# A gated recurrence with a highway layer behind it: loads with four instead of eight neighbouring tokens per partition, and another written order

## The chip, the cores and the metric

The kernel runs on one core of one Trainium2 chip. The metric is the device time of one execution in microseconds (us). Before the change the median of three runs is 213.28 us (213.11 to 213.91).

## What is computed

Four sequences of 6,336 tokens with 256 features go through a gated recurrence and then, token by token, through a highway layer:

```
f = lb + (1 - lb) * sigmoid(f_logit)          # lb: one number a feature
h[t] = f[t] * h[t-1] + (1 - f[t]) * x[t]      # one recurrence for each sequence and feature
H = max(h @ w_h, 0);  T = sigmoid(h @ w_t + b_t)
out = T * H + (1 - T) * h                     # [4, 6336, 256] as 25344 rows, float32
```

All inputs and the output are float32 in memory: 26 MB each for x, f_logit and out.

## The kernel before

The work is cut into 25 units. Each of units 0 to 23 is 1,024 tokens (8 blocks of 128) of one sequence; the last one, unit 24, is 192 tokens of each of the four. Units 0 to 2 and 24 enter in smaller pieces (`CUTS`, line 44), so that there are 30 front pieces and 26 back pieces. Pieces are numbered from 0 below.

**Front**, for each piece i. `lt` and `xt` are loaded with tokens on the partitions (line 106). ScalarE makes `u = sigmoid(-lt)` (line 154). GpSimd makes the product `bv = u * xt`, 256 columns of features for two blocks an instruction (lines 160 and 172). TensorE transposes `u` to `uT` (line 198) and `bv` to `bT` (line 215), so that features lie on the partitions and tokens along them; ScalarE makes the decay `f = 1 + ncc * uT` (line 205); VectorE runs the recurrence as a scan, `y = f * y + bT` (line 230).

**Back**, for each unit. TensorE multiplies `y` by the two weight matrices, to `zp` and `gp` (line 245); ScalarE makes `t` (line 251); VectorE makes `d` (line 256); VectorE and GpSimd share the product `e = d * t` (line 166 on VectorE, line 160 on GpSimd; of backs 0 to 2 VectorE makes all of it); TensorE adds `y` and `e` and transposes back, to `op` (lines 296 and 297); ScalarE copies it to `o` (line 303), and in the last three backs VectorE does part of that. `o` is stored (line 309).

**The weights** are loaded raw (line 125, two loads of 256 KB) and scaled once by VectorE into `w_sb` (line 148, two instructions, h = 0 and h = 1, each over both matrices); each reads both `w_raw` and `ndiag` from SBUF.

**Which tokens a load puts on a partition.** `run(piece)` (line 108) tells how many neighbouring tokens go to one partition. With 8, a partition gets 8 tokens as one piece of 8,192 bytes; with 4, it gets two pieces of 4,096 bytes. Pieces of 4 or 2 blocks have a run of 4 or 2 in any case, and the last unit has 2. Line 205 puts the tokens of `f` back in order as it writes, and line 213 does so for `bT`. Stores always use up to 4 tokens, which is 4,096 bytes.

**What sets the order.** `PLAN` (line 349) is a list written out by hand: each letter issues the next step of its kind, and the engines get their instructions in that order. L and X load `lt` and `xt`, Q loads a weight, U is `u`, P the GpSimd product, A and B the transposes of `u` and `bv`, F the decay, S the scan, W the scaling of the weights, Z and G the matrix products, T, D and E the gates and the VectorE part of `e`, H the GpSimd part of it, O the output transposes, C and V the copies on ScalarE and VectorE, R the store. The digit after A, B, Z, G or O is the PSUM slot. All loads and stores go through SyncE's queue in the list's order. In what follows S2.0 is the scan of front piece 2, half 0, W0 and W1 are the two instructions of line 148, and so on. The buffers of `lt` and `xt` are 5 each, those of `o` 8.

Where VectorE makes `e`, the next GpSimd product is made to wait for it (`port`, line 156). Line 148 has no such wait.

Of the kernel before, what the change touches and what calls it, by code (L numbers as in the profile page):

```python
# [19 lines left out]
def kernel(  # L20
# [36 lines left out]
    units = [(P, NB, b, NB, s0) for s0 in range(0, S - rest, NB * P) for b in range(B)]  # L57
# [44 lines left out]
    def load(i, name, src):  # L102
        u, j0, j1 = fronts[i]
        np_, j = units[u][0], run(fronts[i])
        t = fs[i][name] = new(name, [NB, D], FP32)
        pin(nc.sync.dma_start(t[:np_, :j1 - j0].rearrange("p (k j) d -> p k (j d)", j=j), tokens(src, u, j0, j1, j)))

    def run(piece):

        u, j0, j1 = piece  # L110
        return min(8, j1 - j0, units[u][3])

    def shape(piece):

# [86 lines left out]
    def decay_act(i, h):  # L201

        np_, N, j = shape(fronts[i])[0], width(fronts[i]), run(fronts[i])
        f = fs[i]["f", h] = new("f", [NB * P], FP16)
        pin(nc.scalar.activation(f[:, :N].rearrange("p (k q j) -> p k q j", q=np_, j=j),  # L205
                                 fs[i]["uT", h].rearrange("p (k j q) -> p k q j", q=np_, j=j), AF.Identity,
                                 scale=ncc[:, h:h + 1], bias=1.0))

    def b_pe(i, m, slot):
        (np_, nb), r = shape(fronts[i]), run(fronts[i]) // 2  # L210
        for bT, h in filled(fronts[i], m, slot, fs[i], "bT", BF16):

            t = bT.bitcast(FP32).rearrange("p (k q j) -> p k j q", q=np_, j=r)
            for k in range(nb // 2):
                pin(nc.tensor.transpose(t[:, k // r, k % r],  # L215
                                        fs[i]["bv"][:np_, k, h * P:(h + 1) * P].rearrange("p d j -> p (d j)").bitcast(FP32),
                                        ident_f[:np_, :np_]))
# [97 lines left out]
    def halves_of(pieces):  # L315
# [31 lines left out]
    }  # L347

    PLAN = (
        "XLLLXXLXLQQUUA0A1PFFFUFUB0PSSB1A0FFPSSPB1A0XLLXLXXPFUFSSWWPB1A0G0Z1PFFUPSSDPXLLXLB0A1G2Z0PUTFFTPPB1S"  # L350
        "SDUSSEZ1A0G0G2A1DDPFTFFPPZ1A0B1O0O2PSSTFECCUB0Z1B1G0G2SDSDA0Z0TUFTPPPPPPA0G1B1FXLLLXRRXLXDESA0Z0Z2O1"
        "UFTCTB0G0A1O1O2SDPPPFCCB1A0Z1G0O2FTUCB0G1PPPHPSDSEDPA1Z0Z2B0O1FTUCTESA1G0G1B0DDHPPPPSZ2O0O1FUTCCB1SA"
        "0G2Z0B1FDUTPHPPSXXLRLRRRLRXLRRZ1A0G2O0PDTFCEEG1B1A0O2O0UFCCDSG1B0A1Z2Z0SDPHPPPPFTTA1B0O2O1G0HPSFCCZ2"
        "B1A0Z1DUTFTEG0O2PSPLXXRXRRRRDPPHCB1SA0O1G0Z2B1FCUTDEPSG1Z0A0O2FTCPDPPHB1A0Z1G0O2SFTCDEB0Z1A1G0PLLXRR"
        "RRSDPPPUFTO2B0A1Z0G1SHDCFTEO2B0G0Z1A1PPPPCUFTSDHO2B0A1G0Z1SCFTO2B0A1DEPSZ1G0PPPCUFTDHO2B0A1O0G1SCFCD"
        "EZ2B0A1Z0PSTFTPPPG1B1O2A0O0DUCFCSG1Z2A1B0HDELXLLRXRLLRXRRRRRXPSTFPPZ1G0O2B1DTCSZ1G2A0O0PHUFTCDEB1A0G"
        "2Z1O0PSPFTCDPPHB0G1G2A1Z0UFTSA0B1FDEDSPO1O0Z2B0PPCCTPHSO1A1G0Z2B0UFTCDEPSA1G0Z2O1PPDB0FTCSA1Z2G0O1PH"
        "FUCTDELXRRXXRRLRLXXRRRA1B0G0Z1PSFTO2DCB1A0G1Z0O2PPPHSUFCTDEB1A0Z1G2O0PSDFTCB0A1Z1G2SFPPPHDO0B1A0G2ET"
        "UCFPSO1PZ0CDTB1A0Z1G2SFTUHO0A0B1DFG1EPPPPSO2A0CCZ0DFB1O2Z1B0TCUTSESHPPG0A1Z2G1DDRRRRRRRRFFTA1B0O2Z0Z"
        "1FCFSEHTTG2B1G0O1RSDDCO2SRHCZ0G1STRO2TDDEZ0CTERTG1O2O0DVDVCO2CREVO1CRO0RCVRR"  # L360
    )
    assert all(PLAN.count(k) == len(places) for k, (_, places) in kinds.items())
    todo = {k: iter(places) for k, (_, places) in kinds.items()}
# [31 lines left out]
```

## Time and profile before

| | |
|---|---|
| median of three runs | 213.28 us |
| the profiled execution | 213.28 us |
| its span, first to last instruction | 211.4 us |
| VectorE (DVE) busy | 195.3 us, 154 instructions |
| ScalarE (ACT) busy | 193.6 us, 194 instructions |
| TensorE (PE) busy | 186.1 us |
| GpSimd (POOL) busy | 160.9 us |
| moved by DMA | 78.69 MB |

The profile is of one execution. "Busy" is time in which an engine had an instruction running; consecutive instructions of VectorE and ScalarE overlap by about 0.1 us, so that the distance between two starts is a little less than a duration. The profiled execution's time is 1.9 us longer than its span. The profile lists instructions by line, engine and tile, and gives for each group what ended the idle time of the engine before it.

### The profile page before, as it was taken

The page shows a single profiled execution, that of the slowest core. Times are in us where ns is not written, and L with a number is a line of the kernel's source. Part 1 is how long each engine was busy: PE and PEld are TensorE (multiplying, and loading weights), DVE is VectorE, ACT ScalarE, POOL GpSimd, SP SyncE. Part 2 cuts the span into 40 slices and gives each one's busy share as a digit, 9 for nine tenths or more (in the row PEclk, how much of TensorE's full clock was granted, in tenths as well). Part 3 has the DMA queues.
Part 4 walks back from the last instruction along what each step waited for, and adds up shares of the span by engine and source line. Part 5 has one row for each costly group of instructions (what it writes and reads, how often), then busy time and mean ns, then how long its engine had stood idle before and what let it go on. Part 6 is the DMA issues. An engine that isn't in the chain of part 4 may idle for free.

```text
span 211.4 us, 4591 instructions
## 1 busy us (share of the span) xinstructions
PE 186.1 (88%) x1775; PEld 131.5 (62%) x1800; DVE 195.3 (92%) x154; ACT 193.6 (92%) x194; POOL 160.9 (76%) x133
## 2 busy tenths in 40 slices
PE   0559988899898999999999999999999899999980
PEld 0336564477565766776767666668576676865770
DVE  1279999999999999999999999999999999999980
ACT  3677999999999999999999999999999999998750
POOL 4667665988699698978988898898899876866400
PEclk9999999999999999999999999999999999999996
DMA  5999999999999999999999999999999996252465
GB/s 124 414 412 429 430 423 425 426 419 426 425 422 425 415 429 419 425 428 414 425 420 428 422 426 420 423 412 426 418 431 409 360 408 282 98 203 99 198 253 198
DMA packets 17350, 78.69 MB, mean 372 GB/s; under 512 B 2352, under 2 KB 2864, under 8 KB 11952
## 3 DMA queue, kind: packets, MB, share of 16 engines
q1 hardware_dynamic: 16784, 78.39, 90.6%
q8 instruction: 14, 0.23, 0.4%
q10 hardware_dynamic: 544, 0.00, 0.1%
q14 instruction: 8, 0.07, 0.1%
HBM read 52.43 MB, written 25.95 MB: 371 GB/s over the span
## 4 chain that ended last, share of the span: by engine, by line
ACT 36%; PE 25%; issue 13%; DVE 13%; DMA 9%; SPq 1%; POOL 1%; ACTq 1%; DVEq 0%; POOLq 0%
ACT t L251 10%; ACT u L154 9%; ACT f L205 8%; ACT o L303 8%; PE zp L245 7%; DMA out_dram<-o 6%; DVE y L230 6%; PE gp L245 6%; DVE d L256 5%; PE bT L215 4%; PE uT L198 3%; PE op L296 3%; DMA xt<-in_x_dram 3%; PE op L297 3%; DVE e L166 1%
## 5 line engine op out<-in xcount | busy, mean ns | idle before, releaser
L160 POOL TENSOR_TENSOR bv<-u,xt 128x512 bf16<-128x512 f16 (+1 forms) x100 | 114.5, 1176 | 30.7 <-DVE e L166 10.3
L230 DVE TENSOR_TENSOR_SCAN y<-f,y,bT 128x1024 bf16<-128x1024 f16 (+3 forms) x56 | 106.4, 1917 | 2.3 <-ACT f L205 1.3
L205 ACT ACTIVATE f<-uT,ncc 128x1024 f16<-128x1024 f16 (+3 forms) x60 | 65.8, 1109 | 2.4 <-PE uT L198 2.4
L251 ACT ACTIVATE t<-zp,bt 128x1024 bf16<-128x1024 f32 (+1 forms) x52 | 63.7, 1247 | 0.7 <-PE zp L245 0.3
L256 DVE SCALAR_TENSOR_TENSOR d<-y,ncc,gp 128x1024 bf16<-128x1024 bf16 (+1 forms) x52 | 62.4, 1209 | 0.3 <-issue 0.2
L245 PEld LDWEIGHTS <-w_sb 128*128 128x128 f16 x400 | 38.0, 99 | 37.6 <-issue 5.8
L303 ACT COPY o<-op 128x1024 f32<-128x1024 f32 (+2 forms) x50 | 55.6, 1157 | 4.2 <-PE op L297 2.2
L154 ACT ACTIVATE u<-lt 128x2048 f16<-128x2048 f32 (+3 forms) x30 | 53.3, 1779 | 4.2 <-DMA lt<-in_f_logit_dram 4.2
L245 PE MATMUL gp<-y,w_sb 128*128 128x512 bf16 (+1 forms) x187 | 50.6, 382 | 1.5 <-ACT t L251 0.2
L245 PE MATMUL zp<-y,w_sb 128*128 128x512 bf16 (+1 forms) x188 | 49.6, 378 | 1.7 <-DVE d L256 0.6
L296 PE MATMUL op<-diag,y 128*128 128x128 f16 (+1 forms) x400 | 49.2, 219 | 1.9 <-DVE d L256 0.7
L160 POOL TENSOR_TENSOR e<-d,t 128x1024 bf16<-128x1024 bf16 x21 | 44.8, 2132 | 7.4 <-DVE e L166 2.6
L297 PE MATMUL op<-ident_b,e 128*128 128x128 bf16 (+1 forms) x400 | 49.2, 219 | 0.0
L297 PEld LDWEIGHTS <-e 128*128 128x128 bf16 (+1 forms) x400 | 44.7, 114 | 5.6 <-issue 3.4
L296 PEld LDWEIGHTS <-y 128*128 128x128 bf16 (+1 forms) x400 | 44.8, 114 | 2.7
L198 PE MATMUL uT<-ident_h,u 128*128 128x128 f16 (+1 forms) x400 | 32.2, 226 | 9.2 <-ACT u L154 6.4
L198 PEld LDWEIGHTS <-u 128*128 128x128 f16 (+1 forms) x400 | 27.3, 101 | 16.4 <-ACT u L154 6.7
L215 PE MATMUL bT<-ident_f,bv 128*128 128x128 f32 (+1 forms) x200 | 32.3, 284 | 5.0 <-DVE y L230 2.4
L215 PEld LDWEIGHTS bT<-ident_f,bv 128*128 128x128 f32 (+1 forms) x200 | 22.9, 145 | 11.5 <-issue 4.6
L166 DVE TENSOR_TENSOR e<-d,t 128x1024 bf16<-128x1024 bf16 (+2 forms) x26 | 18.9, 734 | 0.1
L230 DVE TENSOR_TENSOR_SCAN y<-f,bT 128x512 bf16<-128x512 f16 (+2 forms) x8 | 10.5, 1338 | 3.3 <-PE bT L215 3.3
L135 DVE TENSOR_SCALAR cc<-lb 128x2 f32<-128x2 f32 x1 | 0.2, 170 | 4.2 <-DMA lb<-in_lower_bound_dram 4.2
(19 smaller groups left out, 10.9 us busy)
## 6 DMA issues: line engine op xcount, KB each, us to landing
out_dram<-o SPq DMA_DIRECT2D x48, 512.0 KB, 13.6
lt<-in_f_logit_dram SPq DMA_DIRECT2D x21, 1024.0 KB, 14.8
xt<-in_x_dram SPq DMA_DIRECT2D x21, 1024.0 KB, 15.8
lt<-in_f_logit_dram SPq DMA_DIRECT2D x5, 512.0 KB, 7.9
xt<-in_x_dram SPq DMA_DIRECT2D x5, 512.0 KB, 8.2
lt<-in_f_logit_dram SPq DMA_DIRECT2D x2, 384.0 KB, 13.0
xt<-in_x_dram SPq DMA_DIRECT2D x2, 384.0 KB, 11.5
xt<-in_x_dram SPq DMA_DIRECT2D x2, 256.0 KB, 4.4
```

Of the source, the lines that this page charges most:

```text
L154: pin(nc.scalar.activation(u[:np_, :nb], fs[i]["lt"][:np_, :nb], AF.Sigmoid, scale=-1.0))
L160: ins = pin(nc.gpsimd.tensor_mul(out_, a, b))
L198: pin(nc.tensor.transpose(uT[:, j * np_:(j + 1) * np_], fs[i]["u"][:np_, j, h * P:(h + 1) * P], ident_h[:np_, :np_]))
L205: pin(nc.scalar.activation(f[:, :N].rearrange("p (k q j) -> p k q j", q=np_, j=j), fs[i]["uT", h].rearrange("p (k j q) -> p k q j", q=np_, ...
L215: pin(nc.tensor.transpose(t[:, k // r, k % r], fs[i]["bv"][:np_, k, h * P:(h + 1) * P].rearrange("p d j -> p (d j)").bitcast(FP32), ident_ ...
L230: pin(nc.vector.tensor_tensor_scan(y, fs[i]["f", h][:, c:c + w], fs[i]["bT", h][:, c:c + w], 0.0 if prev is None else prev, op0=ALU.mult, ...
L245: pin(nc.tensor.matmul(p[:, a:e], w_sb[:, k, ki, h * P:(h + 1) * P], y_of(j)[:, ki, a:e], start=ki == 0, stop=ki == NH - 1))
L251: pin(nc.scalar.activation(bs[j]["t"][:, m, :width(backs[j])], bs[j]["zp", m], AF.Sigmoid, bias=bt[:, m:m + 1]))
L256: pin(nc.vector.scalar_tensor_tensor(bs[j]["d"][:, m, :width(backs[j])], y_of(j)[:, m], ncc[:, m:m + 1], bs[j]["gp", m], op0=ALU.mult, op1 ...
L296: pin(nc.tensor.matmul(o, y[:, h, cols], diag[:, h], start=True, stop=False))
L297: pin(nc.tensor.matmul(o, bs[j]["e"][:, h, cols], ident_b, start=False, stop=True))
L303: pin(copy(bs[j]["o", q][:np_, a:e], bs[j]["op", q][:np_, a:e]))
```

## The change

The run of a load goes from 8 to 4, and the order list is another one. In units 3 to 23, the ones of eight blocks in one piece, each load becomes two pieces of 4,096 bytes a partition instead of one of 8,192. Nothing else in the code differs; the scaling of the weights (line 148) and the share of `e` (line 263) are the same lines in both.

```diff
     def run(piece):
         u, j0, j1 = piece
-        return min(8, j1 - j0, units[u][3])
+        return min(4, j1 - j0, units[u][3])
...
-        "XLLLXXLXLQQUUA0A1PFFFUFUB0PSSB1A0FFPSSPB1A0XLLXLXXPFUFSSWWPB1A0G0Z1PFFUPSSDPXLLXLB0A1G2Z0PUTFFTPPB1S"
...
+        "XLLLXXLUUA0A1PFFFFUB0PSSA1B0FUFPSSPA0B1XQQLXLXLLXPPWFFUSSWB0A1PFUFPSSPXXLLXLG0Z1B0A1Z2PTFUFTPPG1B1DS"
...
```

The head of the list, engine by engine:

| | before | after |
|---|---|---|
| SyncE's queue | X0 L0 L1 L2 X1 X2 L3 X3 L4 Q0 Q1 X4 L5 L6 X5 L7 X6 | X0 L0 L1 L2 X1 X2 L3 X3 Q0 Q1 L4 X4 L5 X5 L6 L7 X6 |
| ScalarE | U0 U1 F0.0 F0.1 F1.0 U2 F1.1 U3 F2.0 F2.1 F3.0 U4 F3.1 F4.0 F4.1 U5 U6 T0.0 | U0 U1 F0.0 F0.1 F1.0 F1.1 U2 F2.0 U3 F2.1 F3.0 F3.1 U4 F4.0 U5 F4.1 T0.0 |
| VectorE | S0 S1 S2.0 S2.1 W0 W1 S3.0 S3.1 D0.0 | S0 S1 W0 S2.0 S2.1 W1 S3.0 S3.1 D0.0 |
| GpSimd | P0 P1 P2.0 P2.1 P3.0 P3.1 P4.0 P4.1 | the same |

Later, every engine has the same instructions as before, in an order that differs here and there by one or two places; the queue of loads and stores differs most. VectorE's order is the same from S22.0 on (147 us in the trace of before) and ScalarE's in the last 20 us; the PSUM slots there have other numbers.

More of the change, by code (lines that the diff above doesn't have):

```diff
@@ L349 @@
     PLAN = (
-        "XLLLXXLXLQQUUA0A1PFFFUFUB0PSSB1A0FFPSSPB1A0XLLXLXXPFUFSSWWPB1A0G0Z1PFFUPSSDPXLLXLB0A1G2Z0PUTFFTPPB1S"
[L351 to L359, printed above, removed]
@@ L360 @@
-        "1FCFSEHTTG2B1G0O1RSDDCO2SRHCZ0G1STRO2TDDEZ0CTERTG1O2O0DVDVCO2CREVO1CRO0RCVRR"
+        "XLLLXXLUUA0A1PFFFFUB0PSSA1B0FUFPSSPA0B1XQQLXLXLLXPPWFFUSSWB0A1PFUFPSSPXXLLXLG0Z1B0A1Z2PTFUFTPPG1B1DS"
+        "SDSSUEA0Z0G1G2A1DDPFTFFPPZ0B0A1O1O2PSSTFECCUB1B0Z0G1G2SDSDA1Z1TUFTPPPPPPA1G0B0FLXRLXRXLXLDESA1O1Z2Z0"
+        "UFCTTB1G1A0O2O0SDPPPFCCB0A1Z2G1O0FTUCB1G2PPHPPSDSEDPA0Z1Z0B1O2FTTUCESG1A0G0B1DDHPPPPSO2Z1O0UFTCCB0SA"
+        "1G1Z2B0FDUTHPPPSRXLRLXLRRRRZ0G1A1O2PDETFCEG0B0O1A1O2UFCCDSG0B1A0Z1Z2SDHPPPPPFTTA0B1O1O0G2HPSFCCZ1B0Z"
@@ new lines @@
+        "0A1DUTFTEG2O1PSPXRXXRRRRLLDPPHCB0SA1Z2G0O1B0FTCDEPSA1G2Z0O1UFTCPDPPHB0A1G2Z0O1SFTCDEB1A0Z0G2PXRRLRRX"
+        "XRLLSDPPFTUO1A0B1G0Z2ESDCFTO1B0A1Z2G0HPPPPPCFTUSDHO1A1B0G2Z0SCFTO1A0B1DEPSZ0G2PPPCFTUDHO1B0A1G0O2SCF"
+        "CDEZ1A0B1Z2PSTFTPPPG0O1A0B1O2DCFCUSG1B0Z0A1Z2HDERRRRXRRLXXLRXLRPSTFTPPPO1G0B1A0G2DCUFSZ1O0B1A0HTCDEZ"
+        "2G1O0PSPFTDPPHB0A1Z2CFTUSG1B1O0G2A0CFDESDPO1Z0A0B1PPCTPHSO1G2Z0B1FUTCDEPSA0Z2G0O1PPPDB1FTCSG2Z0A0O1H"
+        "UFCDEXXLRRRLLXXRRRRRLB1A0Z2G1PSTTFO0DCB1A0Z2G1O0PPHSFUCTDEB0A1G1Z0O2PPSDFTCB1A0G0SFPPHDO1A0B1Z2G0EUC"
@@ L361 @@
+        "TFPPSO1PZ2CDTB0A1Z1G0SFTUHO2A1B0DFG1EPPPPSO0A1CCZ2DFB0Z0O1B1TTCUSESHPPG2A0Z0G1DDRRRRRRRRFFTB0A1O0Z2Z"
+        "1FCFSEHTTG0B1G2O1RSDDCO0SRHCZ2G1STRO0TDDEZ2CTERTG1O0O2DVDCO0CVEVRO1CRO2RCVRR"
     )
```

## The prediction

> **What bounds the kernel now.** I read the page first: engines, then slices.
>
> ```profile
> PE 186.1 (88%) x1775; PEld 131.5 (62%) x1800; DVE 195.3 (92%) x154; ACT 193.6 (92%) x194; POOL 160.9 (76%) x133
> ...
> DVE  1279999999999999999999999999999999999980
> ACT  3677999999999999999999999999999999998750
> ...
> DMA  5999999999999999999999999999999996252465
> GB/s 124 414 412 429 430 423 425 426 419 426 425 422 425 415 429 419 425 428 414 425 420 428 422 426 420 423 412 426 418 431 409 360 408 282 98 203 99 198 253 198
> ```
>
> Three resources are full at once: VectorE and ScalarE from 16 us to about 195 us, the DMA engines from 5 us to about 170 us. A resource that is busy all the time need not be the bound, so the next view is who waits. VectorE's waits between 20 and 205 us are these, all of them:
>
> ```profile
> DVE y L230 <- PE bT L215: 0.4, 1, 0.4
> DVE o L303 <- PE op L297: 0.4, 2, 0.2
> DVE d L256 <- issue: 0.2, 1, 0.2
> ```
>
> That is 1.0 us in 185 us. VectorE runs from its first gapless instruction, S3.0 at 17.61 us, to the end almost without a hole, and what it has to do after that is the same in both kernels. ScalarE has 11.0 us of distance beyond its shortest intervals, of which 4.9 us lie before 20 us and 4.1 us after 190 us, where it waits for VectorE's and TensorE's tail. So a delay of S3.0 is a delay of the end; a delay of a load is one only after its slack is used up.
>
> **Part 1: loads in pieces of 4,096 bytes.** No engine's instruction gets longer. The decay at line 205 reads and writes with another inner length; its start-to-start distance is 0.995 us for 1,024 columns with a run of 8, and 0.569 us for 512 columns with a run of 4, in the pieces that have it already. The difference is 0.83 ns a column, as from 1,024 to 2,048 columns of `u` (0.946 to 1.800 us): the run is not paid for. Products, scans and stores are untouched.
>
> The DMA may get slower. In the trace's packet records a packet of 4,096 bytes takes 159 ns and one of 8,192 takes 309 ns. There are 5,376 of the large ones, so 5,376 x (318 - 309) ns / 16 engines = 3.0 us more DMA time. Against this stand two stretches, the first with loads of 4,096 bytes almost alone, the second with 8,192 alone:
>
> ```profile
> 15.00:20.00 5.00, 4.15 (x18) 2.69 (x20) 5.00 (x6) 3.66 (x6) 2.83 (x3) 1.00 1.04 430
> 25.00:30.00 5.00, 4.24 (x32) 2.44 (x32) 5.00 (x5) 5.00 (x6) 2.26 (x3) 1.00 1.00 424
> ```
>
> 430 GB/s against 424: at the packet level the small ones overlap, and nothing is lost (the DMA would even gain 1.4%). A third row, 408 GB/s where small pieces and stores are mixed (160 to 165 us), would cost 44 million bytes x (1/408 - 1/424) = 4.1 us. I take 1.9 us, from landings in a row: 2.455 us for 1 MB of load in 8,192 bytes, 2.50 us for 1 MB of stores in 4,096 bytes, over the 42 loads that change (44 million bytes).
>
> What hides it: the lead of a load's landing over the `u` that needs it. Before, L8, L9 and L10 land 2.4, 1.5 and 1.4 us ahead, L15 2.9 us, all later ones 7 us and more. Adding up the new queue's bytes at these rates, with the 2.8 us by which real landings trail such a sum, L8 to L10 keep about 1 us, L13 2.3, L15 3.3, L18 1.8, the rest over 5. X10 lands 0.9 us before its product, other `xt` earlier. The `o` buffers come free 1.6 us or more before their copies. So the cost is 0; without this cover, up to 1.9 us, with the worst row 4.1 us.
>
> **Part 2: the head of the list.** Here the change moves something that VectorE pays for. W0 now stands ahead of S2.0, the weights' loads ahead of L4. The trace on line 148:
>
> ```profile
> L148 DVE SCALAR_TENSOR_TENSOR w_sb<-o,cc x2: 727/1190/1654, 15.4 to 16.0; 128x512 f16<-128x512 f32 x2
> L148 DVEq EVENT_SEMAPHORE  x1: 21/21/21, 14.6 to 14.6; - x1
> ```
>
> Two equal instructions, one of 0.73 us, one of 1.65 us. What GpSimd did beside them tells why:
>
> ```profile
> 15.39 0.73 DVE L148 SCALAR_TENSOR_TENSOR w_sb<-o,cc 128x512 f16<-128x512 f32 x1
> ...
> 16.04 1.65 DVE L148 SCALAR_TENSOR_TENSOR w_sb<-o,cc 128x512 f16<-128x512 f32 x1
> ...
> 12.09 2.29 POOL L160 TENSOR_TENSOR bv<-u,xt 128x512 bf16<-128x512 f16 x2 [0.16 <-POOL bv L160]
> 15.94 1.20 POOL L160 TENSOR_TENSOR bv<-u,xt 128x512 bf16<-128x512 f16 x1 [1.57 <-DMA xt<-in_x_dram]
> ```
>
> W0 ran while GpSimd was idle. W1 started 0.10 us after P4.0, and ended 0.55 us after P4.0's end (17.14 to 17.69); P4.1, issued at 17.11 while W1 waited, took 1.61 us in place of 1.16. The two do not share, one stands still.
>
> The new head, step by step. The semaphore row says that the second weight load is in at 14.6 us. It now has one load of 512 KB less ahead of it (1.24 us by the landings), so 13.35 us; W0, behind S1.1 (done at about 12), starts at 13.37. P3.0 and P3.1 stand where they stood (12.09 to 14.38: L3, X3 and U3 are unmoved), so P3.1 is running, and W0 ends 0.55 us after it, at 14.93. The next start comes 0.08 us earlier: S2.0 at 14.85, S2.1 at 16.02, W1 at 17.19 (1.17 us each). P4.0 runs from 15.94 (X4 lands at 15.8 either way), P4.1 from 17.06 to 18.22. W1 is 0.13 us late, waits for all of P4.1, ends at 18.77, and S3.0 starts at 18.69 in place of 17.61: **+1.08 us**. ScalarE shares the fate: A4 needs the slot that S2.1 frees and T0.0 the weights, so U7 moves from 24.3 to about 25.5, and no slack of ScalarE's takes the 1.08 back. Behind W1 are queued all scans, and D0.0, for which the back of unit 0 waits.
>
> The page "SBUF — State Buffer" of the Trainium skill (Who interferes with whom) says that a VectorE instruction with two SBUF inputs and a GpSimd instruction that reads SBUF exclude each other whole, the first to issue winning. By it both blocks are whole, as above; if they shared instead, each W would lose about half of a 1 us overlap, and the sum would be near -0.62 + 1.0 = +0.4.
>
> Bounds of this part: if neither meets a product, each W takes 0.64 us from start to start and S3.0 begins at 13.37 + 0.64 + 2 x 1.17 + 0.64 = 16.99 us, -0.62. If each costs the full difference of the two rows, 0.93 us, it is -0.62 + 1.86 = +1.24. I take the value that follows GpSimd's own times, 1.08.
>
> **Part 3: the other moves.** They change nothing in amount. VectorE's distances beyond the shortest hold 1.8 us between 50 and 120 us (0.5 at 75 us, where a scan waits for `bT`, 0.3 at 81 us); the order around S12.1, F12.1 and U15 is the same in both. I take 0, between -1.8 (all gone) and +1.8 (as much again).
>
> **The sum**, on the profiled execution's 213.28 us (span 211.4 and 1.9 around it; it equals the median): 0 + 1.08 + 0 gives 214.36, say **214.4 us**.
>
> **Rivals.**
> *A. Only W0 is blocked.* If W1 is issued 0.13 us sooner, it waits in front of P4.1, as in the trace of before, and goes at 17.14: ends at 17.69, S3.0 at 17.61, as now. 213.3 us, no change: the other side of my forecast. For: 0.13 us is less than the error of a landing. Against: W1's start hangs on W0's end, which P3.1 sets, and P4.1's on the landing of X4; both have their times from before. With neither blocked it is 213.28 - 0.62 = 212.7.
> *B. The DMA becomes the bound.* A step takes VectorE and ScalarE about 7.5 us, and 3 MB at 424 GB/s take 7.4. If the small loads run at the 408 row, 4.1 us less some 2.5 us of slack and the head's delay come on top: 214.4 + 1.6 = 216.0. For: packet durations, mixed row. Against: 430 GB/s.
> *C. The new order closes holes.* 1.8 us less with A's head: 213.3 - 1.8 = 211.5; with part of it, up to 212.2. Against: the largest hole, 0.5 us, stands in an order that is unchanged.
> *D. The change does not do what it is called.* Its label says that GpSimd scales the weights and that VectorE alone makes the first three backs' `e`. Neither is in the diff: line 148 is VectorE's and line 263 the same in both. Were GpSimd to scale, VectorE's chain would lose 2 x 0.64 us more than with neither blocked, 212.66 - 1.28 = 211.4.
>
> **Numbers.** Forecast case 0.40, half of it past +0.5% (about what a measurement of this kernel tells from no change; 1.07 us, so 214.35); A 0.25, nearly all within 0.5%; C 0.13, mostly faster; B and other new waits 0.22, slower. Faster 0.11, same 0.45, slower 0.44. Range: from neither-blocked, with a little of C, to B, which leaves out no more than 2 in 10: 212.4 to 216.2. The likeliest case's own range is 213.8 to 215.0.
>
> **What would show it.** Line 148: two instructions of about 1.55 us, starting near 13.4 and 17.2, each ending 0.5 us after a GpSimd product; S3.0 at 18.7. One long and one short, S3.0 at 17.6: A. VectorE waits for line 205 or ScalarE for `lt` between 30 and 110 us, DMA row under 415 GB/s: B. Fewer waits of VectorE: C. The decay must stay at 0.995 us; a longer one would make part 1 wrong.

## The result, and the profile after

The kernel after takes 215.74 us (median of four runs, 214.85 to 215.84), the kernel before beside it 213.22 us (213.11 to 213.91): a ratio of **1.0102** (95% interval 1.0068 to 1.0136), slower by 1.0%. Compared again later, it gave 1.0069 (1.0045 to 1.0092). The forecast was 214.4, the range 212.4 to 216.2. The profiled execution took 215.84 us.

The page of the kernel after, first engines, then slices:

```profile
PE 188.0 (88%) x1775; PEld 131.8 (62%) x1800; DVE 196.4 (92%) x154; ACT 193.8 (91%) x194; POOL 160.4 (75%) x133
...
DVE  1279899999999999999999999999999999999970
ACT  3774899999999999999999999999999999997750
...
GB/s 147 410 410 419 423 419 419 421 415 423 416 416 422 420 416 419 417 421 415 419 422 415 421 417 419 419 418 420 416 420 269 397 413 310 109 188 101 196 281 165
```

The middle is as full as it was. The DMA row is a little lower (415 to 423 in slices 4 to 30, where it was 412 to 431, with one slice of 269 near 163 us), and no engine waits for a load behind 20 us. The fifth slice of VectorE, 21.4 to 26.8 us, has lost its 9, and ScalarE's fourth and fifth stand at 4 and 8. So the head is the place to look. VectorE there, in order of time:

```profile
13.27 1.61 DVE L148 SCALAR_TENSOR_TENSOR w_sb<-o,cc 128x512 f16<-128x512 f32 x1 [1.11 <-DMA o<-in_moe_w_h_dram]
14.81 2.44 DVE L230 TENSOR_TENSOR_SCAN y<-f,y,bT 128x512 bf16<-128x512 f16 x2
17.17 1.45 DVE L148 SCALAR_TENSOR_TENSOR w_sb<-o,cc 128x512 f16<-128x512 f32 x1
18.54 2.32 DVE L230 TENSOR_TENSOR_SCAN y<-f,bT 128x512 bf16<-128x512 f16 x2
20.78 1.25 DVE L256 SCALAR_TENSOR_TENSOR d<-y,ncc,gp 128x1024 bf16<-128x1024 bf16 x1
22.77 2.45 DVE L230 TENSOR_TENSOR_SCAN y<-f,y,bT 128x512 bf16<-128x512 f16 x2 [0.74 <-issue]
```

Both instructions of line 148 are long (1.61 and 1.45 us, forecast about 1.55), start at 13.27 and 17.17 (13.37 and 17.19), and S3.0, the fourth line, starts at 18.54 (18.69). That is the forecast. The last line is not in it: before S4.0 VectorE stands still for 0.74 us, and S4.0 is now 1.60 us later than the 21.17 of before.

**A ruler for the head.** The first loads land at a different time in every execution (X4 at 15.63 to 17.45 us in the profiles of this study), and all that follows moves with them: S0.0 starts 7.2 to 7.5 us ahead of X4's landing in every profile. So starts are counted from X4's landing here, as the trace's completions give it. The middle and the tail are the stretch from S4.0's start to that of VectorE's last instruction, V25.1. Each row is one execution, while the ratio is that of all runs of its comparison; it is not quite the quotient of two medians. The runs of one kernel scatter: before took 213.11 to 215.80 us in the four comparisons (medians 213.22 to 214.19), and its profile, 213.28, is one of the fastest.

| kernel (order list, edit) | line 148, us | S3.0 | S4.0 | S4.0 to V25.1 | ratio |
|---|---|---|---|---|---|
| before | 0.73, 1.65 | 1.83 | 5.39 | 184.31 | 1 |
| before's list, run of 4 | 0.72, 1.65 | 1.82 | 5.45 | 184.32 | 1.0022 |
| after | 1.61, 1.45 | 2.91 | 7.14 | 185.62 | 1.0102 |
| after, again | 0.75, 0.77 | 1.80 | 6.34 | 185.67 | 1.0069 |
| after's list, run of 8 | 0.75, 0.77 | 1.81 | 6.48 | 185.51 | 1.0114 |
| after, old tail | 1.74, 1.36 | 2.95 | 6.39 | 184.91 | 1.0094 |
| after, ndiag in PSUM | 0.75, 0.72 | 1.76 | 6.20 | 185.63 | 1.0101 |
| after, TensorE kept busy | 0.75, 1.19 | 1.79 | 5.21 | 185.28 | 1.0071 |
| after, PSUM + old tail | 0.74, 0.72 | 1.75 | 6.57 | 184.78 | 1.0078 |
| after, busy + old tail | 1.69, 1.43 | 2.91 | 6.33 | 184.89 | 1.0038 |
| after, all three | 0.75, 0.72 | 1.32 | 4.73 | 184.70 | 0.9962 |
| before, busy | 0.72, 0.75 | 0.96 | 4.38 | 185.03 | 0.9988 |
| before, PSUM + busy | 0.72, 0.74 | 0.95 | 4.37 | 185.21 | 0.9959 |

By this ruler the first profile of after loses 1.75 us up to S4.0 and 1.31 behind it. Note rows 4 and 7: with line 148 short, S3.0 is as early as in before, and S4.0 is late all the same.

**The hole before S4.0.** S4.0 reads the transposes B4. TensorE in the kernel after:

```profile
17.39 1.01 PE L198 MATMUL uT<-ident_h,u 128*128 128x128 f16 x8 [1.58 <-DVE y L230]
18.20 1.91 PE L245 MATMUL gp<-y,w_sb 128*128 128x512 bf16 x4
19.90 0.63 PE L245 MATMUL zp<-y,w_sb 128*128 128x512 bf16 x1
20.76 1.06 PE L245 MATMUL zp<-y,w_sb 128*128 128x512 bf16 x2 [0.22 <-issue]
21.61 1.06 PE L215 MATMUL bT<-ident_f,bv 128*128 128x128 f32 x4
22.46 0.77 PE L198 MATMUL uT<-ident_h,u 128*128 128x128 f16 x8
23.07 1.03 PE L245 MATMUL zp<-y,w_sb 128*128 128x512 bf16 x4
```

The chain is A4 (which waits for S2.1, the end of its slot's last use), G0.0, Z0.0 (four matmuls, of which one is missing from the trace's records), B4: it ends at 22.67, D0.0 on VectorE had ended at 22.03. Look also at the pace: four matmuls of 512 columns take 1.91 us at 18.20 and 1.03 us at 23.07. They start 0.43 us apart up to some moment, and 0.22 us apart from then on. The same stretch in the kernel before:

```profile
15.63 1.09 PE L215 MATMUL bT<-ident_f,bv 128*128 128x128 f32 x4 [1.61 <-DVE y L230]
16.51 1.06 PE L198 MATMUL uT<-ident_h,u 128*128 128x128 f16 x8
17.36 1.91 PE L245 MATMUL gp<-y,w_sb 128*128 128x512 bf16 x4
...
20.47 0.60 PE L215 MATMUL bT<-ident_f,bv 128*128 128x128 f32 x4
```

And VectorE beside it, in before:

```profile
19.86 1.25 DVE L256 SCALAR_TENSOR_TENSOR d<-y,ncc,gp 128x1024 bf16<-128x1024 bf16 x1
21.17 2.45 DVE L230 TENSOR_TENSOR_SCAN y<-f,y,bT 128x512 bf16<-128x512 f16 x2
```

There B4 ends at 21.07 and D0.0 at 21.11: the two chains were already level, to 0.04 us. From S2.1's end at 15.48 TensorE, with B3, A4, G0.0, Z0.0 and B4, needed 5.6 us, and VectorE, with W0, W1, S3.0, S3.1 and D0.0, 5.6 us as well. The change takes one link out of each: W0 (0.64 us from its start to W1's) now stands ahead of S2.0, and B3 (0.88 us from its start to A4's) has another slot and no longer waits for S2.1. VectorE's chain falls to 4.8 us, but TensorE's only to 5.4, because its slow pace lasts longer: from G0.0's start to B4's end it is 4.47 us, after 3.71 in before.

That the pace opens the hole shows in a kernel of the experiments below, "old tail", which has the same head. There line 148 is blocked twice as well, but TensorE turns fast sooner, by chance:

```profile
18.88 1.91 PE L245 MATMUL gp<-y,w_sb 128*128 128x512 bf16 x4
20.58 1.46 PE L245 MATMUL zp<-y,w_sb 128*128 128x512 bf16 x4
21.88 0.60 PE L215 MATMUL bT<-ident_f,bv 128*128 128x128 f32 x4
```

From G0.0's start to B4's end it is 3.60 us, B4 ends at 22.48, D0.0 at 22.62, and there is no hole.

**The tail.** From the list of waits of the kernel after (us in total, times, longest), VectorE's from 20 us on:

```profile
DVE o L303 <- ACT o L303: 0.6, 1, 0.6
```

And ScalarE's from 190 us on:

```profile
ACT o L303 <- DVE o L303: 2.6, 2, 1.8
```

The first row is new, and the second is 2.0 us in three waits in before: VectorE's copy V23.1 waits for ScalarE's copy C23.1, which now stands ahead of it in the list and writes to the same tile of `o`; ScalarE does C23.0 first. VectorE's own order did not change; what changed is which engine's step is named first.

### The profile page after: what moved, and what is told of

Read it like the earlier page. It is cut to its first block, busy times and chain, and to the rows that moved or that the text cites. A ratio compares the mean times of both kernels' runs of the same rounds, so it can differ in the third digit from the quotient of the medians.

```text
span 214.1 us, 4586 instructions
## 1 busy us (share of the span) xinstructions
PE 188.0 (88%) x1775; PEld 131.8 (62%) x1800; DVE 196.4 (92%) x154; ACT 193.8 (91%) x194; POOL 160.4 (75%) x133
## 4 chain that ended last, share of the span: by engine, by line
PE 38%; ACT 35%; issue 11%; DVE 7%; DMA 5%; SPq 0%; ACTq 0%; DVEq 0%
ACT t L251 11%; PE zp L245 9%; PE gp L245 9%; ACT u L154 9%; ACT f L205 8%; ACT o L303 8%; PE uT L198 6%; PE bT L215 5%; PE op L297 5%; PE op L296 5%; DMA o<-in_moe_w_h_dram 3%; DVE d L256 3%; DVE y L230 2%; DMA lt<-in_f_logit_dram 2%; DVE e L166 1%
## 5 line engine op out<-in xcount | busy, mean ns | idle before, releaser
L251 ACT ACTIVATE t<-zp,bt 128x1024 bf16<-128x1024 f32 (+1 forms) x52 | 62.5, 1245 | 1.5 <-PE zp L245 1.2
L303 ACT COPY o<-op 128x1024 f32<-128x1024 f32 (+2 forms) x50 | 55.0, 1145 | 4.6 <-DVE o L303 2.6
L297 PE MATMUL op<-ident_b,e 128*128 128x128 bf16 (+1 forms) x400 | 49.7, 219 | 0.6 <-DVE e L166 0.6
L215 PE MATMUL bT<-ident_f,bv 128*128 128x128 f32 (+1 forms) x200 | 32.9, 289 | 2.2 <-POOL bv L160 1.0
L148 DVE SCALAR_TENSOR_TENSOR w_sb<-o,cc 128x512 f16<-128x512 f32 x2 | 3.1, 1528 | 1.1 <-DMA o<-in_moe_w_h_dram 1.1
```

Source lines behind the costliest of these rows:

```text
L215: pin(nc.tensor.transpose(t[:, k // r, k % r], fs[i]["bv"][:np_, k, h * P:(h + 1) * P].rearrange("p d j -> p (d j)").bitcast(FP32), ident_ ...
L251: pin(nc.scalar.activation(bs[j]["t"][:, m, :width(backs[j])], bs[j]["zp", m], AF.Sigmoid, bias=bt[:, m:m + 1]))
L297: pin(nc.tensor.matmul(o, bs[j]["e"][:, h, cols], ident_b, start=False, stop=True))
L303: pin(copy(bs[j]["o", q][:np_, a:e], bs[j]["op", q][:np_, a:e]))
```

## The experiments

**The list and the run, one at a time.** First the new list with loads of 8 tokens, then the old list with loads of 4:

```diff
-        return min(4, j1 - j0, units[u][3])
+        return min(8, j1 - j0, units[u][3])
```

> The changed kernel's order list, with loads of 8 neighbouring tokens as before. Theory 1 (the order does it: 1.6 us by the head up to S4.0, 0.4 us between 40 and 57 us, 0.7 us in the tail; the size of the loads' pieces costs nothing): 215.7 us, the same as the changed kernel within 0.4 us, and S4.0 at 22.8 us. Theory 2 (the smaller pieces slow the DMA, and the order only follows): 213.3 to 214.0 us, with S4.0 near 21.2.

Measured: 216.39 us, ratio 1.0114 (1.0090 to 1.0138). The time is 0.7 above the 215.7 expected, but the runs of before beside it were higher too (median 214.03). The loss is there with loads of 8.

```diff
-        return min(8, j1 - j0, units[u][3])
+        return min(4, j1 - j0, units[u][3])
```

> The order list of before, with loads of 4 neighbouring tokens. Theory 1 (the order does it): 213.2 us, the same as before within 0.4 us, S3.0 at 17.6 us, and no wait of ScalarE for lt after 20 us although the DMA moves about 417 GB/s in place of 421. Theory 2 (smaller pieces slow the DMA): 214.5 to 215.7 us, with ScalarE or GpSimd waiting for loads.

Measured: 214.53 us, ratio 1.0022 (1.0002 to 1.0042). S4.0 and the middle stand where they stood in before, to 0.06 us. So nearly the whole loss is the list's; the loads in smaller pieces cost nothing that a trace shows, and at most 0.4% in the times, whose interval lies just above 1.

**Old head, new rest.** The first 98 steps of before's list, then after's.

> Loads of 4; the first 98 steps of the list (to about 27 us, up to E0 and D1.1) are those of before, the rest those of the changed kernel. Theory 1: the head's 1.6 us come back: 214.1 us, S4.0 at 21.2 us, and what remains is the 0.4 us of the middle and the 0.7 us of the tail. Theory 2 (the loads do it): 215.7 us. Theory 3 (a delay in the head is made good later, where VectorE waits for bT): 215.0 us or more, S4.0 at 21.2 but the end hardly moved.

Measured: 216.65 us, ratio 1.0123 (1.0097 to 1.0149). S3.0 is where it was in before (1.82), S4.0 nearly (5.72 after 5.39), but S4.0 to V25.1 takes 186.34 us, 0.7 more than in after: the seam opens holes of its own, 0.42 us before 33 us and 0.31 before 44 us, beside one of 0.41 before S4.0. The 214.1 us of theory 1 did not come, and the run says nothing on what a better head is worth.

**Old tail.** The last 17 steps in before's order, V23.1 ahead of C23.0 and C23.1:

```diff
-        ...O2DVDCO0CVEVRO1CRO2RCVRR"
+        ...O2DVDVCO0CREVO1CRO2RCVRR"
```

> The changed kernel with the last 17 steps in the order of before: V23.1 ahead of C23.0 and C23.1 in the list, instead of behind them. Each engine's own order stays the same. Theory 1 (both copies write one tile, so the list's order makes one wait for the other): V23.1 no longer waits 0.6 us for ScalarE's copy, 215.0 us. Rival (the last copies don't set the end, the shift of 0.7 us at V23.1 is given back by the store): 215.7 us.

Measured: 215.81 us, ratio 1.0094 (1.0065 to 1.0122). The time alone can't tell, its interval holds 1.0102; the trace can. VectorE in after:

```profile
204.88 0.60 DVE L256 SCALAR_TENSOR_TENSOR d<-y,ncc,gp 128x384 bf16<-128x384 bf16 x1
206.10 0.69 DVE L303 COPY o<-op 128x512 f32<-128x512 f32 x1 [0.62 <-ACT o L303]
206.71 0.55 DVE L166 TENSOR_TENSOR e<-d,t 128x768 bf16<-128x768 bf16 x1
```

And in this kernel:

```profile
204.68 0.60 DVE L256 SCALAR_TENSOR_TENSOR d<-y,ncc,gp 128x384 bf16<-128x384 bf16 x1
205.21 0.68 DVE L303 COPY o<-op 128x512 f32<-128x512 f32 x1
205.81 0.55 DVE L166 TENSOR_TENSOR e<-d,t 128x768 bf16<-128x768 bf16 x1
```

From D25.1 to V23.1 it is 1.22 us in the one and 0.53 in the other; S4.0 to V25.1 falls from 185.62 to 184.91. The tail's 0.7 us is shown in the trace.

**The second SBUF input of line 148.** `ndiag` goes to a PSUM slot that is not used until line 148 is done, and VectorE clears it:

```diff
-    ndiag = new("o", [2, NH, D], FP32)
-    nc.gpsimd.memset(ndiag, 0.0)
+    ndiag = psum("2", [2, NH, D], "ndiag", FP32)
+    nc.vector.memset(ndiag, 0.0)
```

> The kernel after, with ndiag in a PSUM slot instead of SBUF (VectorE clears it), so that line 148 reads one SBUF input and one PSUM input; everything else is as in the kernel after. Theory 'VectorE stands still beside GpSimd's products only because line 148 has two SBUF inputs, and this sets S3.0': both instructions of line 148 take about 0.73 us beside a running product instead of 1.61 and 1.45; S2.0 then waits for its transposes and starts near 14.0 instead of 14.8, S3.0 near 17.0 to 17.6 instead of 18.5 (relative to S0.0 at 8.3); A4, G0.0 and B4 move up by 0.85 us with S2.1; the time falls by 0.9 to 1.5 us against the kernel after, to a ratio of 1.003 to 1.006. Rival 'the length of line 148 does not matter, TensorE's order and pace in the head set S4.0': line 148 gets short, S3.0 comes earlier, but S4.0 stays within 0.4 us of 22.8 and the ratio at 1.009 or more. Rival 'it is the memory of w_sb or the write that blocks, not the second SBUF input': line 148 keeps about 1.5 us.

Measured: 216.33 us, ratio 1.0101 (1.0074 to 1.0127): **no gain**. Line 148 is line 152 of this kernel:

```profile
14.60 0.75 DVE L152 SCALAR_TENSOR_TENSOR w_sb<-o,cc,ndiag 128x512 f16<-128x512 f32 x1 [0.94 <-DMA o<-in_moe_w_h_dram]
15.77 2.45 DVE L230 TENSOR_TENSOR_SCAN y<-f,y,bT 128x512 bf16<-128x512 f16 x2 [0.41 <-PE bT L215]
18.13 0.72 DVE L152 SCALAR_TENSOR_TENSOR w_sb<-o,cc,ndiag 128x512 f16<-128x512 f32 x1
18.77 2.32 DVE L230 TENSOR_TENSOR_SCAN y<-f,bT 128x512 bf16<-128x512 f16 x2
21.12 1.28 DVE L256 SCALAR_TENSOR_TENSOR d<-y,ncc,gp 128x1024 bf16<-128x1024 bf16 x1
23.21 2.45 DVE L230 TENSOR_TENSOR_SCAN y<-f,y,bT 128x512 bf16<-128x512 f16 x2 [0.81 <-PE bT L215]
```

Both are short. S3.0 stands at 1.76 us behind X4's landing, where before has 1.83. What follows is the rival's course: the time that VectorE gains is handed to the hole before S4.0 (0.81 us), as B4 is not done.

**TensorE kept busy.** Matmuls that compute nothing of the result, into a PSUM slot not yet in use; the loop stands in the step that issues A, ahead of its transposes:

```diff
+    heat = ps1.tile([P, NB * P], FP32, tag="two1", name="heat")
+    HEAT = {0: 36, 1: 4, 2: 10, 3: 10, 4: 14}
...
+        for _ in range(HEAT.get(i, 0) if m == 0 else 0):
+            pin(nc.tensor.matmul(heat[:, :P], ident_b, ident_b, start=True, stop=True))
```

> The kernel after with idle-filling TensorE matmuls that compute nothing of the result: 128x128 products of ident_b into a PSUM slot not yet in use, 36 ahead of A0, 4 ahead of A1, 10 ahead of A2, 10 ahead of A3 and 14 ahead of A4. Theory 'TensorE runs at half pace until it has been busy for some us, and this opens the 0.74 us hole before S4.0': matmuls of line 245 start 0.22 us apart from the first one on instead of 0.43, B4 ends before D0.0 does, S4.0 follows D0.0 without a hole, S3.0 stays near 18.5 (relative to S0.0 at 8.3) as line 148 is still blocked; the time falls by 0.5 to 1.0 us against the kernel after (ratio 1.005 to 1.008). Rival 'the slow matmuls are a matter of what runs beside them, weights just written or DMA': line 245 still starts at 0.43 us distance before 22 us, the hole stays, the ratio stays at 1.010 or gets worse by the fillers.

Measured: 215.52 us, ratio 1.0071 (1.0047 to 1.0095). Line 245 runs at 0.22 us from its first matmul on, but for one distance of 0.36, the hole is gone, S4.0 stands at 5.21. In this execution one instruction of line 148 was blocked for part of its time, the other not at all. It was the fastest of the eight runs (214.17 us), and the ratio is no better than that of the kernel after compared again (1.0069, below). So the trace shows the pace and the closed hole; a gain in time from this edit alone is not shown.

> The kernel before with the same idle-filling matmuls (36, 4, 10, 10 and 14 ahead of A0 to A4). In the kernel before there is no hole behind S3.0, whose start is set by the blocked second instruction of line 148 (it ends 0.55 us after P4.0). Theory 'pace of TensorE': the bT and uT transposes get shorter by 0.3 to 0.5 us each, S1.1 and S2.0 come 0.3 to 0.8 us earlier; if W1 then starts before P4.0 (near 15.9) it wins the race, S3.0 moves to 16.6 to 16.9 and the time falls by 0.6 to 1.0 us (ratio 0.995 to 0.997); if it does not, S3.0 stays and the ratio is 1.000. Rival 'pace is not by warmth': nothing moves, ratio 1.000 to 1.003.

Measured: 213.68 us, ratio 0.9988 (0.9968 to 1.0008). In the profile W1 starts 0.55 us ahead of P4.0 and is not blocked, S4.0 comes 1.0 us earlier, and 0.7 us of that is lost again, most of it by 57 us, where loads and products stand where they stood. So the 0.995 to 0.997 expected for a W1 that wins the race did not come. The profiled run was one of the slowest of the twelve (214.52 us).

**Two losses undone.** ndiag in PSUM and the old tail:

> The kernel after with two of its losses undone at once: ndiag in PSUM (line 148 not blocked) and the last 17 steps in the order of before (V23.1 ahead of C23.0 and C23.1). If the losses are independent and add up, the time falls by 0.7 us for the tail and by 0.9 to 1.5 us for the head: ratio 0.999 to 1.003 against the kernel before. If the head's gain is eaten by TensorE's pace, ratio 1.006 to 1.008.

Measured: 215.45 us, ratio 1.0078 (1.0053 to 1.0104): in the trace the tail's part came (184.78), the head's did not (S4.0 at 6.57, a hole of 1.2 us before it).

**The same kernel once more.**

> The kernel after itself, unchanged, beside the experiments and on the same chip. All theories: ratio about 1.010. What is asked: how far S4.0 stands behind the landing of the load X4, which is 7.14 us in the first profile of this kernel and 5.39 in the kernel before. If line 148's wait for GpSimd and TensorE's slow matmuls are the cause, the distance is 6.2 to 7.2 us again, near 6.4 where only one of the two instructions of line 148 is blocked.

Measured: 216.05 us (215.01 to 216.98, 12 runs), ratio 1.0069 (1.0045 to 1.0092). The profile is the best witness of the study, since here line 148 won both races against GpSimd by chance, in the unchanged kernel:

```profile
14.22 0.75 DVE L148 SCALAR_TENSOR_TENSOR w_sb<-o,cc 128x512 f16<-128x512 f32 x1 [0.95 <-DMA o<-in_moe_w_h_dram]
15.38 2.45 DVE L230 TENSOR_TENSOR_SCAN y<-f,y,bT 128x512 bf16<-128x512 f16 x2 [0.40 <-PE bT L215]
17.75 0.77 DVE L148 SCALAR_TENSOR_TENSOR w_sb<-o,cc 128x512 f16<-128x512 f32 x1
18.44 2.32 DVE L230 TENSOR_TENSOR_SCAN y<-f,bT 128x512 bf16<-128x512 f16 x2
20.73 1.28 DVE L256 SCALAR_TENSOR_TENSOR d<-y,ncc,gp 128x1024 bf16<-128x1024 bf16 x1
22.98 2.45 DVE L230 TENSOR_TENSOR_SCAN y<-f,y,bT 128x512 bf16<-128x512 f16 x2 [0.97 <-PE bT L215]
```

W0 starts 0.06 us ahead of P3.1, W1 0.18 us ahead of P4.1. S3.0 is as early as in before (1.80 after 1.83), yet this execution took 216.12 us: S4.0 waits 0.97 us for B4.

**The two causes of the head, apart and together.**

> The kernel after with two losses undone: the idle-filling matmuls ahead of A0 to A4, and the last 17 steps in the order of before. Line 148 may still be blocked by GpSimd's products. If the tail's 0.7 us and the pace of TensorE add up: 0.7 us less than with the idle-filling matmuls alone, ratio 1.002 to 1.006. If the tail's gain only shows while the head is late, ratio 1.007.

Measured: 215.29 us, ratio 1.0038 (1.0015 to 1.0061). In the profile line 148 was blocked twice, and A4 came so late that TensorE, which had run at the fast pace from 13.2 us on, stood idle for 1.7 us before it and went at the slow pace again until 21.6 us. So the added matmuls did not do all they were meant to here; B4 still ended a little ahead of D0.0, and there was no hole.

> The kernel after with three losses undone: idle-filling matmuls, the tail's order of before, and ndiag in PSUM, so that line 148 is not blocked. If these three are all that the new list costs, S4.0 stands at 4.4 to 5.5 us behind X4's landing as in the kernel before, and the ratio is 0.998 to 1.003. Against the same kernel without ndiag in PSUM, this one shows what line 148's wait costs once TensorE is not slow: 0.3 to 1.1 us if the wait is on the path, 0 if the head is bound by the loads and TensorE. Rival 'something else in the new list, its queue of loads or the pieces of 4,096 bytes, holds the middle': ratio 1.005 or more with V25.1 more than 0.7 us later, counted from S4.0, than in the kernel before.

Measured: 213.73 us (213.45 to 214.15), ratio **0.9962** (0.9946 to 0.9979). This is below the 0.998 to 1.003 expected. VectorE, line 148 being line 154 here and the lines behind it four higher than in after:

```profile
17.16 0.72 DVE L154 SCALAR_TENSOR_TENSOR w_sb<-o,cc,ndiag 128x512 f16<-128x512 f32 x1
17.80 2.33 DVE L234 TENSOR_TENSOR_SCAN y<-f,bT 128x512 bf16<-128x512 f16 x2
20.04 1.25 DVE L260 SCALAR_TENSOR_TENSOR d<-y,ncc,gp 128x1024 bf16<-128x1024 bf16 x1
21.21 2.44 DVE L234 TENSOR_TENSOR_SCAN y<-f,y,bT 128x512 bf16<-128x512 f16 x2
```

No hole is left, and TensorE's chain beside it goes at the fast pace:

```profile
17.39 0.61 PE L202 MATMUL uT<-ident_h,u 128*128 128x128 f16 x8 [0.76 <-DVE y L234]
18.05 0.81 PE L249 MATMUL gp<-y,w_sb 128*128 128x512 bf16 x3
18.70 1.03 PE L249 MATMUL zp<-y,w_sb 128*128 128x512 bf16 x4
20.27 0.63 PE L219 MATMUL bT<-ident_f,bv 128*128 128x128 f32 x4 [0.55 <-DVE y L234]
```

S4.0 in after's list, us behind X4's landing, by what VectorE met on the way (the profile in which one instruction of line 148 was blocked in part, 5.21, is left out):

| | waits for B4 | B4 in time |
|---|---|---|
| line 148 blocked twice | 7.14 | 6.39; 6.33 |
| line 148 free | 6.20 to 6.57 (four profiles) | 4.73 |

These are not two costs in a row. While B4 is late, freeing line 148 brings 0.6 to 0.9 us; where B4 is in time, it brings 1.6, of which 0.4 goes with the fast pace (S3.0 at 1.32 instead of 1.76, as S2.0 waits for transposes). And with line 148 blocked, a B4 in time brings no more than the 0.75 us of the hole. Two chains run side by side from S2.1 to S4.0, and the later one counts. Each cell but one holds one or two executions.

**The best of it on before's list:**

> The kernel before with ndiag in PSUM and the idle-filling matmuls: a version that may beat both kernels. With W1 at 0.73 us instead of 1.65 and S3.0 not held by its transposes, S3.0 moves up by 0.9 us to 0.9 us behind X4's landing. If VectorE's head is on the path of the end, the ratio is 0.995 to 0.997; if the middle takes it back because loads and products stand where they stood, 0.998 to 1.000.

Measured: 213.63 us (213.40 to 213.91), ratio **0.9959** (0.9940 to 0.9977). This and the kernel with all three edits beat both kernels of the case by about 0.4% and can't be told from each other. S4.0 gains 1.0 us, the middle gives most of it back in the profile (185.21 after 184.31).

This pair is the fairest test of the causes. Without the edits the two lists took 216.05 and 214.19 us in this comparison; with `ndiag` in PSUM and the added matmuls in both, and before's tail in both, they took 213.73 and 213.63. So nearly all that parts the lists lies in these three things.

## Why the prediction was right and where it was not

- **Direction and S3.0: right, with some luck.** Slower, with the first loss in the head. In the profiled execution the working of part 2 held step by step; S3.0 was put 1.08 us later, and counted from X4's landing it is 1.08 (2.91 less 1.83). But line 148 lost both races in only three of six profiles of after's list with `ndiag` in SBUF, and its wait is not what makes the list slow: with line 148 free the list still took 216.33 us (`ndiag` in PSUM) and 216.12 (the repeated execution).
- **The time: inside the range, outside the likeliest case's own.** 215.74 us is above the 213.8 to 215.0 of the forecast case. It falls where the range was kept open for rival B and "other new waits", and it was the latter.
- **Loads cost nothing: right as far as the runs tell.** 1.0022 with the old list, which leaves room for up to 0.4%; the decay's distance stayed at 0.995 us. The leads were larger than worked out (L8 to L10 land 4.5, 4.8 and 3.3 us ahead of their `u` in after). Rival B is out.
- **The middle's holes unchanged: right.** The wait for `bT` near 75 us (0.40 us in before's trace, 0.43 in after's) and the one near 81 us (0.20 in both) are there as before.
- **"So a delay of S3.0 is a delay of the end": the step that failed.** It read the head as one chain, VectorE's. The prediction names A4 and the slot that S2.1 frees, but costs them at the same 1.08 (U7, put at about 25.5 us, started at 26.37). Between S2.1 and S4.0 a second chain runs on TensorE, level with VectorE's to 0.04 us in before, and both start at S2.1, which the new list moves by 1.5 us even when line 148 is free (its end is 0.30 us ahead of X4's landing in before and 1.19 us behind it in the repeated run). The prediction did not look at TensorE's pace either: in after the slow pace reaches through Z0.0 and B4, so TensorE's chain stays long although B3 has left it, while VectorE's is shorter by W0. Size at S4.0: 1.75 instead of 1.08.
- **Rival A's price was wrong, its race is real.** The margin of 0.13 us does fall either way: of six profiles of after's list with ndiag in SBUF, three had line 148 blocked twice, two not at all, and one had one of its instructions blocked for part of its time. But a race won does not give "as now, 213.3": the execution that won both took 216.12.
- **"They change nothing in amount": wrong in the tail.** Each engine's order in the last steps is the old one, but a step's place against another engine's decides who waits at a shared tile: +0.71 us.
- **Part 3's zero: off by 0.6 us in the middle.** 185.62 less 184.31 less 0.71. About half of it is again a VectorE instruction beside a GpSimd product: E2, the product `e` of back 2. VectorE in before:

```profile
41.90 1.21 DVE L166 TENSOR_TENSOR e<-d,t 128x2048 bf16<-128x2048 bf16 x1
```

In after:

```profile
43.65 1.43 DVE L166 TENSOR_TENSOR e<-d,t 128x2048 bf16<-128x2048 bf16 x1
```

And GpSimd in after:

```profile
39.47 4.54 POOL L160 TENSOR_TENSOR bv<-u,xt 128x512 bf16<-128x512 f16 x4
```

In after a product still runs, to 44.01, when E2 starts (0.22 us more); in before the last one had ended at 41.91. E3 has 0.10 more. The dependence at line 156 holds back the next product, not one that has begun. The rest, steps of 0.1 to 0.2 us near 42 and 164 us, was not followed.
- **The sum.** 1.75 (to S4.0) + 1.31 (middle and tail), less 0.15 for loads that landed earlier and 0.35 behind V25.1's start (0.10 of it outside the span), is the 2.56 us between the two profiled executions; the forecast had 1.08 of it.

The run with 214.85 us among the four of the first comparison has no profile; whether it won the race, turned fast early or only had early loads stays open.

## What to carry to other kernels

Before costing a delay at the instruction that suffers it, list every chain that ends at the next meeting point and its margin there; where two chains are level, freeing one buys little. An instruction that is moved changes the chains on its own engine, and the same list may change those of another, so add up each anew, here W0's and B3's. Look at several executions where a race of 0.1 us decides. When an order list is compared, compare it across engines wherever two of them write parts of one tile, not engine by engine.

## What the runs showed of the hardware that was not expected

- **TensorE starts at half pace.** Matmuls of 512 columns start 0.43 us apart until 20.2 to 23.6 us into every kernel without the added matmuls, then 0.22; the transposes of `u` go from 0.11 to 0.055 us. The row of the granted clock shows 1.00 in both stretches, so it doesn't tell them apart. The turn comes at a different moment in each execution: 20.2 us in before, 21.4 to 23.6 us in six profiles of after's list. Over all nine such profiles it came 3.4 to 5.4 us after TensorE's last idle stretch of 1 us or more. It can be undone: in the kernel with the old tail and the added matmuls, 1.7 us of idleness came between the fast pace and the slow one.
- The Trainium skill, page "TensorE: Matmul & The Clock Gate" (Part 1: The HAM clock gate), states start distances of 426.7 and 215.7 ns for 512 columns at its two clocks, a turn after about 3.4 us of sustained work in a free-running window, and that its moment varies from run to run. The traces here agree with both distances and with the varying moment; none of them measures the window by itself.
- **An input in PSUM frees VectorE from GpSimd.** With ndiag in PSUM, seven of the eight instructions of line 148 in four profiles overlapped a GpSimd product; they took 0.72 to 0.75 us and the products 1.16 to 1.17. With ndiag in SBUF one of the two gave way wherever they ran beside each other for 0.5 us or more: line 148 took up to 1.74 us, or the product up to 1.72. The Trainium skill, page "SBUF — State Buffer" (Who interferes with whom), ties the exclusion to two inputs in SBUF, and these runs agree.
- **The start varies by almost 2 us.** X4 landed at 15.63 to 17.45 us in the profiles, and all starts moved with it, so that two profiles of one kernel are compared by distances from that landing, not by starts.
